# Squares for an overflow check, and the high parts of split numbers, given to other engines and other places in a planned kernel

## The chip, the cores and the metric

The kernel runs on one core of a Trainium2 chip. The core has TensorE (PE), VectorE (DVE), ScalarE (ACT) and GpSimd (POOL), and SyncE (SP), whose queue issues nearly all DMAs here. The metric is the device time of one execution in microseconds.

## The reference

Attention with capped scores for 4 batches of 12 heads, 448 positions and 64 features, and then a gated two-layer product on its output, all in fp32:

```python
scores = scale * np.matmul(q, k.transpose(0, 1, 3, 2))
scores = cap * np.tanh(scores / cap)
attn = softmax(scores)                   # along the keys, 1e-9 added to the sum
x = (attn @ v) as [1792 tokens, 768]
g, val = x @ w_gate, x @ w_val           # [768, 1536]
out = (g * sigmoid(g) * val) @ w_out     # [1536, 768]
```

## The kernel before, in words

Three stages follow each other on TensorE.

*Attention.* 24 pairs of heads, two pairs (a quad) at a time. Per quad TensorE makes seven score tiles in PSUM (`sc`, L884), ScalarE takes tanh (L888) and exp (L891) of each, VectorE adds up (L811, L813), and TensorE multiplies by v (`av`, L829, L910) and sums (L916). The result is copied out of `av` (op `xk`) and later multiplied by reciprocals that travel through DRAM (ops `rl`, `rs`, `rld`; the last is L838 on SP, the product L847 on VectorE, op `x`). That is x, cut into blocks B11, B21, B22 and so on for two halves w of the batches.

*Expert products.* The products are done by a seven-product scheme (p = 1, 2, 6, 5, 7, 3, 4) over sums and differences of blocks. Every fp32 operand is split into a high fp16 part (a cast, ops `XH` for x and `wH` for weights, L259 on VectorE or L257 on ScalarE) and a low one (`XL`, `wL`: the number minus its high part, L264 on VectorE), and each product is three fp16 matmuls (L527 high by high, L528, L529). There are 13 steps over 12 column blocks f; the first has only w = 0, the last only w = 1. Per step ScalarE or VectorE copy banks out of PSUM (`c1`, `cu`, `c5`; tiles c00 to c21), VectorE adds others (`c11`, `c22`, `c12`, L545), ScalarE takes silu (L560, tile `th`), VectorE makes the gated value (`va`, L565), and SP stores it (`hst`, L571, tensor `hidden`).

*Output products.* The gated values are loaded back (`hld`, L614) and go through the same scheme with w_out in two passes (pr = 0, 1), with `oH`, `oL`, `wH`, `wL` as above and matmuls at L702 to L704; L723 adds a bank to a tile, L727 stores the output.

Beside this, ScalarE squares x, the gate weights, w_out and the gated values (op names `qx`, `q`, `qo`, `qh`, all by L322, with the row maximum check `fit` at the end): a check that no fp16 part over- or underflows. Only that check reads the squares.

The order of the instructions on every engine is set beforehand by a planner (class Plan). Each op has a priority, the engines that may do it with a supposed duration on each, the ops it depends on, and the buffers it takes, with the ops that set them free. The planner steps through supposed time, takes the ready op of the best priority, and picks the engine that ends first. So a dependency that is dropped, or an engine that is forbidden, reorders the program around it. A queue works in its order; what stands behind a waiting instruction waits too.

Of the kernel before, what the change touches and what calls it, by code (L numbers as in the profile page):

```python
# [16 lines left out]
P = 128  # L17
# [62 lines left out]
class Plan:  # L80
# [9 lines left out]
    ISSUE = {"rld": 0.96}  # L90
    LAND = {}
    BIAS = {}
# [12 lines left out]
    def run(self):  # L105
# [69 lines left out]
        while ready:  # L175
# [20 lines left out]
            if e == "SP":  # L196
                b = max(s + 1.125, dma_free)
                free[e] = s + self.ISSUE.get(k[0], 0.48)
                dma_free = b + d
                end[k] = dma_free + 0.73 + self.FAR.get(k[0], 0.0)  # L200
            else:
                free[e] = s + d
                end[k] = s + d
                end[k] += self.LAND.get(k[0], 0.0)
                if e == "PE":
                    last = kind(k)
# [17 lines left out]
def tile_capped_attention_gated_mlp(ctx: ExitStack, tc: tile.TileContext, qd, kd, vd, cap, eye, w1, w2, out):  # L224
# [198 lines left out]
    def blocks(w):  # L423
        g0, g1 = 2 * w * NCC, (2 * w + 1) * NCC
        for c in range(HALF):
# [14 lines left out]
            for p, (_, _, _, z) in PROD.items():  # L440

                def high(e, z=z, c=c):
                    T["xs", z, w, c] = x_half(("XH", z, w, c), home(z, w, c))
                    copy(e, T["xs", z, w, c][:, 0], T["raw", z, w, c])

                def low(e, z=z, c=c):
                    sub(e, T["xs", z, w, c][:, 1], T["raw", z, w, c], T["xs", z, w, c][:, 0])

                raw = ("x", {"B11": g0 + c, "B21": g0 + c + HALF, "B22": g1 + c + HALF}[z]) if z[0] == "B" else (z, w, c)
                order = prod_at[w, w, p] - AHEAD + 0.3 * c  # L450
                op(("XH", z, w, c), order, {"ACT": 0.57, "DVE": 0.39} if w else {"DVE": 0.39}, high, [raw], [(home(z, w, c), [("p", LAST[w], w, p)])])
                op(("XL", z, w, c), order + 0.01, {"DVE": 0.62}, low, [("XH", z, w, c)])
                if z in PLAIN:
                    square(("qx", z, w, c), 2, order + 3.0, 0.58, lambda z=z, c=c: T["raw", z, w, c], [raw], ("XH", z, w, c))

    def step(s):
# [46 lines left out]
        for half in range(2):  # L503
            if 0 in ws:
                square(key("q", half), 0, at[0] - 6.0 + 2.0 * half, 0.85, lambda half=half: gate(half).rearrange("p a b -> p (a b)"), full[half], ("XH", "B11", 0, 0))
        last = [2, 5, 3, 4]
        for n in range(4):
            tw = at[n] - 8.8
            k = 1.0 if n < 3 else 0.5
            deps = [full[0], [key("S", 2)], [key("S", 4)], full[1]][n]  # L510
            use = [("p", s, w, last[n]) for w in ws]
            op(key("wH", n), tw, {"ACT": 0.85 * k, "DVE": 0.56 * k}, lambda e, n=n: wH(e, n), deps, [(wtag(4 * s + n), use)])
            op(key("wL", n), tw + 1.0, {"DVE": 0.95 * k}, lambda e, n=n: wL(e, n), [key("wH", n)])

        for w in ws:
# [32 lines left out]
            at_ = lambda p, w=w: done[w, p]  # L548
            op(k("c1"), at_(1), both, lambda e, g=keep: g(e, 0, "b2"), [("p", s, w, 1)], [(f"c0{cw(w)}", [("hst", 2 * w, f)])])
            op(k("c11"), at_(2), {"DVE": 0.62}, lambda e, g=plus: g(0, "b1"), [("p", s, w, 2), k("c1")])  # L550
            op(k("cu"), at_(6), both, lambda e, g=keep: g(e, 1, "b2"), [("p", s, w, 6)], [(f"c1{cw(w)}", [("hst", 2 * w + 1, f)])])
            op(k("c5"), at_(5), both, lambda e, g=keep: g(e, 2, "b3"), [("p", s, w, 5)], [(f"c2{cw(w)}", [key("va", w, 1)])])
# [3 lines left out]
            for b in range(2):  # L556
# [40 lines left out]
    def hslot(pr, i, b, c):  # L597
        users = {
            (0, 0): [("oT", pr, "T4", c), ("oL", pr, 6, c)], (0, 1): [("oT", pr, "T2", c), ("oL", pr, 5, c)],
            (1, 0): [("oL", pr, 4, c)], (1, 1): [("oT", pr, "T2", c), ("oL", pr, 3, c), ("qh", pr, 1, 1, c)],  # L600
        }[i, b]
# [3 lines left out]
    def outs(pr):  # L605
# [15 lines left out]
        for i, b in ((0, 0), (1, 0), (0, 1), (1, 1)):  # L621
            for c in range(HALF):
# [38 lines left out]
        for n, (p, d) in enumerate(OUT_ORDER):  # L661
# [112 lines left out]
    def pair(u, q):  # L774
# [33 lines left out]
        def sadd(e, n):  # L808
# [438 lines left out]
```

## Time and profile before

| | us |
|---|---|
| median of 3 runs | 612.39 |
| lowest and highest | 612.13, 613.45 |
| the profiled execution, as timed | 613.15 |
| its span, first to last instruction | 611.1 |
| TensorE busy in it | 592.3 |
| VectorE, ScalarE busy | 509.6, 405.1 |

The three stages take TensorE to about 168, 460 and 605 us of the span. An engine's busy share is a mean over stages with different limits, so the rows below go by stretches.

### The profile page before, as it was taken

How to read it: one execution, taken by the hardware profiler on the slowest of the kernel's cores; microseconds unless marked ns; L12 is line 12 of the kernel's file. 1: busy time of each engine (PE TensorE's matmuls, PEld its weight loads, DVE VectorE, ACT ScalarE, POOL GpSimd, SP SyncE). 2: the span in 40 equal slices, each digit the busy share in tenths (PEclk: the TensorE clock that was granted, in tenths of full speed). 3: DMA queues.
4: the chain of work that ended last, by engine and by line, in shares of the span. 5: the costliest groups of instructions: out<-in, count | busy, mean ns of one | idle time of the engine just before them, and what ended most of it. 6: DMA issues, size and time to landing. Idle time of an engine off the chain costs nothing.

```text
span 611.1 us, 9532 instructions
## 1 busy us (share of the span) xinstructions
PE 592.3 (97%) x3333; PEld 279.6 (46%) x3333; DVE 509.6 (83%) x878; ACT 405.1 (66%) x669; POOL 1.5 (0%) x11
## 2 busy tenths in 40 slices
PE   7999999999897999999999999999999899999995
PEld 2333333333353455555555555555555455555552
DVE  2779899996998999788989989897969998998830
ACT  6999999999786755545455464452768977953311
POOL 1000000000000000000000000000000000000000
PEclk9999999999999999999999999999999999999998
DMA  8586588664313355878777687767578689644111
GB/s 254 203 243 192 175 232 236 192 171 143 95 40 109 127 168 160 251 221 235 226 242 219 202 248 228 220 200 245 224 248 297 211 285 318 192 147 153 48 61 65
DMA packets 69453, 118.07 MB, mean 193 GB/s; under 512 B 13588, under 2 KB 47380, under 8 KB 69397
## 3 DMA queue, kind: packets, MB, share of 16 engines
q1 hardware_dynamic: 69362, 117.38, 61.8%
q8 instruction: 28, 0.46, 0.3%
q14 instruction: 29, 0.23, 0.1%
q0 software_dynamic: 32, 0.00, 0.0%
q10 hardware_dynamic: 2, 0.00, 0.0%
HBM read 81.79 MB, written 35.48 MB: 192 GB/s over the span
## 4 chain that ended last, share of the span: by engine, by line
PE 90%; DVE 5%; ACT 2%; DMA 1%; issue 1%; SPq 0%; ACTq 0%
PE b L527 10%; PE b L528 10%; PE b L529 10%; PE sc L884 10%; PE av L829 9%; PE b L704 7%; PE b L703 7%; PE b L702 7%; PE om L529 4%; PE om L527 4%; PE om L528 4%; PE b L916 2%; DVE B L264 2%; PE av L910 2%; DMA wf<-w 1%; PE om L704 1%
## 5 line engine op out<-in xcount | busy, mean ns | idle before, releaser
L527 PE MATMUL b<-A,w 128*128 128x448 f16 x252 | 88.8, 353 | 1.8 <-ACT c L257 1.5
L528 PE MATMUL b<-A,w 128*128 128x448 f16 x252 | 88.8, 352 | 1.1 <-DVE w L264 1.1
L529 PE MATMUL b<-A,w 128*128 128x448 f16 x252 | 88.8, 352 | 0.0
L527 PEld LDWEIGHTS <-w 128*128 128x128 f16 x504 | 49.3, 98 | 49.9 <-issue 3.4
L528 PEld LDWEIGHTS <-w 128*128 128x128 f16 x504 | 49.3, 98 | 48.8 <-issue 1.8
L529 PEld LDWEIGHTS <-w 128*128 128x128 f16 x504 | 49.3, 98 | 45.9
L257 ACT ACTIVATE c<-b 128x448 f32<-128x448 f32 x54 | 28.9, 536 | 45.1 <-PE b L704 25.3
L529 PE MATMUL om<-B,w 128*128 128x448 f16 x144 | 50.7, 352 | 0.4 <-DVE B L264 0.4
L527 PE MATMUL om<-B,w 128*128 128x448 f16 x144 | 50.8, 352 | 0.0
L528 PE MATMUL om<-B,w 128*128 128x448 f16 x144 | 50.8, 352 | 0.0
L884 PE MATMUL sc<-c,c 64*128 64x448 f32 (+1 forms) x192 | 44.9, 572 | 1.7 <-ACT w L888 1.7
L264 DVE TENSOR_TENSOR A<-A,A 128x448 f16<-128x448 f32 (+3 forms) x55 | 44.5, 828 | 1.1 <-ACT A L257 0.9
L257 ACT ACTIVATE wf<-w 128x384 f32<-128x384 f32 x37 | 20.7, 559 | 36.7 <-DMA w<-w 35.9
L888 ACT ACTIVATE w<-sc 128x896 f32<-128x896 f32 x42 | 36.9, 918 | 7.8 <-PE sc L884 7.6
L545 DVE TENSOR_TENSOR c<-c,b 128x448 f32<-128x448 f32 x60 | 37.0, 617 | 5.6 <-PE b L529 3.8
L264 DVE TENSOR_TENSOR w<-B,w 128x768 f16<-128x768 f32 x39 | 37.0, 954 | 3.4 <-ACT w L257 3.2
L704 PE MATMUL b<-B,w 128*128 128x448 f16 x108 | 38.1, 352 | 1.8 <-DVE B L264 1.8
L529 PE MATMUL b<-B,w 128*128 128x448 f16 x108 | 38.1, 352 | 1.6 <-DVE B L264 1.6
L888 ACT ACTIVATE B<-sc 128x896 f32<-128x896 f32 x42 | 36.8, 921 | 3.8 <-PE sc L884 3.6
L560 ACT ACTIVATE th<-c 128x448 f32<-128x448 f32 x48 | 26.2, 568 | 18.8 <-DVE c L565 11.4
L891 ACT ACTIVATE B<-B 128x896 f32<-128x896 f32 x42 | 38.3, 959 | 0.1
L891 ACT ACTIVATE w<-w 128x896 f32<-128x896 f32 x42 | 38.2, 956 | 0.0
(134 smaller groups left out, 1240.8 us busy)
## 6 DMA issues: line engine op xcount, KB each, us to landing
w<-w SPq DMA_DIRECT2D x72, 384.0 KB, 3.7
hidden<-c SPq DMA_DIRECT2D x48, 224.0 KB, 2.2
B<-w_S SPq DMA_DIRECT2D x24, 384.0 KB, 3.5
w<-wf SPq DMA_DIRECT2D x16, 384.0 KB, 4.5
B<-w SPq DMA_DIRECT2D x15, 384.0 KB, 5.4
th<-parts SPq DMA_DIRECT2D x48, 112.0 KB, 3.0
A<-hidden SPq DMA_DIRECT2D x12, 448.0 KB, 5.6
B<-hidden SPq DMA_DIRECT2D x12, 448.0 KB, 4.7
```

The costliest lines, as they stand in the source:

```text
L257: nc.scalar.activation(out_, in_, AF.Copy, scale=1.0 if scale is None else scale)
L264: ENG[e].tensor_tensor(out_, a, b, op=ALU.subtract)
L527: nc.tensor.matmul(o, lhsT=wh, rhs=xh, start=first, stop=False, skip_group_check=True)
L528: nc.tensor.matmul(o, lhsT=wl, rhs=xh, start=False, stop=False, skip_group_check=True)
L529: nc.tensor.matmul(o, lhsT=wh, rhs=xl, start=False, stop=end, skip_group_check=True)
L702: nc.tensor.matmul(o, lhsT=wh, rhs=xh, start=first, stop=False, skip_group_check=True)
L703: nc.tensor.matmul(o, lhsT=wl, rhs=xh, start=False, stop=False, skip_group_check=True)
L704: nc.tensor.matmul(o, lhsT=wh, rhs=xl, start=False, stop=end, skip_group_check=True)
L829: nc.tensor.matmul(T["av", u][D * i : D * i + D, :S], lhsT=T["rv", q][:, a : a + D], rhs=t_(own[j])[:, i], start=j == 0, stop=False, skip_ ...
L884: nc.tensor.matmul(z[rows, h, :S], lhsT=T["rk", w][r, keys], rhs=T["rq", w][r], start=True, stop=True)
L888: nc.scalar.activation(T["t", q, i], T["sc", q, i][:, :, :S], AF.Tanh, scale=icapr)
L891: nc.scalar.activation(T["t", q, i], T["t", q, i], AF.Exp, scale=capr)
```

## The change

The squares are taken elsewhere. Those of x read the high parts (fp16) in the middle of the expert products, and no longer hold the fp32 blocks. Those of the gated values are taken from the tiles c right after the gating, 48 half as large ones in place of 24 on what is loaded back, and hold those tiles. Those of the weights of f = 0 are taken in the last step and not in the first; those of w_out in the second output pass and not in the first. The check `fit` stands later. High parts of x for w = 0 may go to ScalarE too; those of the weights of steps 1 and 2 and of the first output pass go to ScalarE alone. The dropped LAND, and ENG[e] made nc.vector, change no instruction.

```diff
-    sq = const.tile([P, 4, 24], F32, name="sq")
+    sq = const.tile([P, 4, 48], F32, name="sq")
...
-        return [], [(tag, [k for y in two for k in [("XL", *y)] + [("qx", *y)] * (y[0] in PLAIN) + [(r, y[1], y[2]) for r in READERS[y[0]]]])]
+        return [], [(tag, [k for y in two for k in [("XL", *y)] + [(r, y[1], y[2]) for r in READERS[y[0]]]])]
...
-                op(("XH", z, w, c), order, {"ACT": 0.57, "DVE": 0.39} if w else {"DVE": 0.39}, high, [raw], [(home(z, w, c), [("p", LAST[w], w, p)])])
+                op(("XH", z, w, c), order, {"ACT": 0.57, "DVE": 0.39}, high, [raw], [(home(z, w, c), [("p", LAST[w], w, p)])])
...
-                    square(("qx", z, w, c), 2, order + 3.0, 0.58, lambda z=z, c=c: T["raw", z, w, c], [raw], ("XH", z, w, c))
+                    n = 3 * PLAIN.index(z) + c
+                    square(("qx", z, w, c), 2, win_at[3] + 10.0 * n + 5.0 * w, 0.58, lambda z=z, c=c: T["xs", z, w, c][:, 0], [("p", 3 + n // 2, 1, 4)], ("XH", z, w, c))
...
-            if 0 in ws:
-                square(key("q", half), 0, at[0] - 6.0 + 2.0 * half, 0.85, ..., full[half], ("XH", "B11", 0, 0))
+            if 1 in ws:
+                square(key("q", half), 0, at[0] - 6.0 + 2.0 * half, 0.85, ..., full[half], ("XH", "B11", s // NFC, 0))
...
-            op(key("wH", n), tw, {"ACT": 0.85 * k, "DVE": 0.56 * k}, ...)
+            op(key("wH", n), tw, {"ACT": 0.85 * k} if s in (1, 2) else {"ACT": 0.85 * k, "DVE": 0.56 * k}, ...)
...
-            op(k("c1"), at_(1), both, ..., [("p", s, w, 1)], [(f"c0{cw(w)}", [("hst", 2 * w, f)])])
+            op(k("c1"), at_(1), both, ..., [("p", s, w, 1)], [(f"c0{cw(w)}", [("hst", 2 * w, f), ("qh", 2 * w, f)])])
...
+                square(("qh", g, f), 3, max(end, z + 2.0) + 1.0, 0.58, lambda b=b, w=w: T["cc", s, w, b], [key("va", w, b)], ("XH", "B11", 0, 0) if s < NFC - 1 else ("oH", 0, 1, 0))
...
-                square(("qh", pr, i, b, c), 3, at[1, 0] + 1.0 + 2.0 * c + (5.0 if i else 0.0), 0.92, ..., [("hld", pr, i, b, c)], ("oH", pr, 2, 0))
...
-            op(("ld", "o", pr, p, d), tp - 24.0, {"SP": 1.09}, load, dep, [(home_, [("wL", "o", pr, p, d)] + [("qo", p, d)] * (not pr))])
-            if not pr:
-                square(("qo", p, d), 1, tp - 6.5, 0.85, ..., [("ld", "o", 0, p, d)], ("oH", 0, p, 0))
+            op(("ld", "o", pr, p, d), tp - 24.0, {"SP": 1.09}, load, dep, [(home_, [("wL", "o", pr, p, d)] + [("qo", p, d)] * pr)])
+            if pr:
+                square(("qo", p, d), 1, tp - 6.5, 0.85, ..., [("ld", "o", 1, p, d)], ("oH", 1, p, 0))
...
-            op(("wH", *key), tp - 7.0, {"ACT": 0.85, "DVE": 0.56}, wH, [("ld", *key)], ...)
+            op(("wH", *key), tp - 7.0, {"ACT": 0.85} if not pr else {"ACT": 0.85, "DVE": 0.56}, wH, [("ld", *key)], ...)
...
-    fit(out_at + len(OUT_ORDER) * 3 * mm_us + 40.0)
+    fit(out_at + len(OUT_ORDER) * 6 * mm_us - 20.0)
```

TensorE's order is the same in both. Lines of the changed file stand one to two lower (L255 is L257 before, L320 is L322).

First, ScalarE at the end of step 0 and the start of step 1: w5, w0 and w2 are high parts of weights, c00 and c20 are copies out of PSUM, sq marks a square. Before:

```order
L257 ACTIVATE B70_1826<-B21_1363 128x448
L257 ACTIVATE c00_1843<-b2_1808 128x448
L322 ACTIVATE B40_1822,sq_76<-B20_1102 128x448
L257 ACTIVATE w5_1850<-ss_1824 128x768
L322 ACTIVATE B70_1826,sq_76<-B21_1363 128x448
L257 ACTIVATE w0_1857<-ss_1838 128x768
L257 ACTIVATE w2_1871<-wf_1847 128x768
L322 ACTIVATE A10_496,sq_76<-wf_1847 128x768
L560 ACT_TABLE_LOAD
L560 ACTIVATE th_1887<-c01_1712 128x448
L322 ACTIVATE A10_496,sq_76<-wf_1855 128x768
L257 ACTIVATE c20_1901<-b3_1875 128x448
```

Now:

```order
L255 ACTIVATE B70_1775<-B21_1362 128x448
L255 ACTIVATE w5_1793<-ss_1769 128x768
L255 ACTIVATE w0_1821<-ss_1773 128x768
L255 ACTIVATE c00_1834<-b2_1809 128x448
L559 ACT_TABLE_LOAD
L559 ACTIVATE th_1850<-c01_1715 128x448
L559 ACTIVATE th_1854<-c11_1747 128x448
L320 ACTIVATE A10_496,sq_76<-c01_1715 128x448
L255 ACTIVATE w2_1874<-wf_1837 128x768
L255 ACTIVATE c20_1888<-b3_1856 128x448
```

The four squares are gone from between, w5 and w0 stand ahead of the copy c00, and a square of a gated value (c01) stands between silu and w2.

Second, VectorE: the high and low parts of x for w = 0, blocks A31, A50 and A51. Before, in the last two quads of attention, among copies out of `av` and block differences:

```order
L264 TENSOR_TENSOR B32_1644<-B50_1232,B30_1225 128x448
L264 TENSOR_TENSOR w4_1639<-wf_1610,w4_1639 128x768
L259 CAST A31_1665<-A51_700 128x448
L264 TENSOR_TENSOR B30_1225<-B30_1225,B12_1095 128x448
L259 COPY c21_1676<-b2_1647 128x224
L259 COPY B31_1472<-av_1615 128x448
L259 COPY B51_1486<-av_1633 128x448
L264 TENSOR_TENSOR A31_1665<-A51_700,A31_1665 128x448
L259 CAST A50_1710<-A52_661 128x448
L259 CAST A51_1714<-A52_661 128x448
L264 TENSOR_TENSOR A50_1710<-A52_661,A50_1710 128x448
L264 TENSOR_TENSOR A51_1714<-A52_661,A51_1714 128x448
```

Now, some 30 us or two quads earlier, behind the sum L812 (L813 before):

```order
L812 TENSOR_TENSOR B72_1380<-B72_1380,w2_1354 128x896
L262 TENSOR_TENSOR A30_1323<-A50_437,A30_1323 128x448
L262 TENSOR_TENSOR A31_1325<-A51_701,A31_1325 128x448
L262 TENSOR_TENSOR A32_1332<-A51_701,A32_1332 128x448
L257 CAST A50_1412<-A52_660 128x448
L257 CAST A51_1416<-A52_660 128x448
L262 TENSOR_TENSOR A50_1412<-A52_660,A50_1412 128x448
L262 TENSOR_TENSOR A51_1416<-A52_660,A51_1416 128x448
L257 CAST B10_1434<-B12_1091 128x448
L257 CAST A52_1436<-w64_1267 128x448
L262 TENSOR_TENSOR B10_1434<-B12_1091,B10_1434 128x448
L262 TENSOR_TENSOR A52_1436<-w64_1267,A52_1436 128x448
```

The conversions and low parts have moved ahead of the last quads' work.

Third, VectorE at the entry into the output products: L723 (now L722) adds the bank `om` to c00, c01 and c10 when the products p = 2, d = 0, 1, 2 are done; B61, B72 and B12 are low parts of the block that product 6 takes. Before:

```order
L723 SCALAR_TENSOR_TENSOR c00_4719<-om_4735,c00_4719 128x448
L264 TENSOR_TENSOR A11_4312<-B62_4564,B11_4545 128x896
L264 TENSOR_TENSOR w1_4774<-B30_4686,w1_4774 128x768
L264 TENSOR_TENSOR B61_4806<-A10_4309,B71_4762 128x896
L723 SCALAR_TENSOR_TENSOR c01_4708<-om_4767,c01_4708 128x448
L264 TENSOR_TENSOR w2_4808<-B31_4698,w2_4808 128x768
L264 TENSOR_TENSOR B40_4547<-B40_4547,A40_4316 128x896
L723 SCALAR_TENSOR_TENSOR c10_4743<-om_4799,c10_4743 128x448
L264 TENSOR_TENSOR A40_4316<-B70_4567,B40_4547 128x896
L264 TENSOR_TENSOR B72_4846<-A11_4312,B41_4797 128x896
L264 TENSOR_TENSOR w3_4842<-B32_4721,w3_4842 128x768
L264 TENSOR_TENSOR B12_4861<-A40_4316,B42_4850 128x896
```

Now:

```order
L262 TENSOR_TENSOR B61_4785<-A10_4347,B71_4762 128x896
L262 TENSOR_TENSOR w0_4777<-B52_4707,w0_4777 128x768
L722 SCALAR_TENSOR_TENSOR c00_4738<-om_4765,c00_4738 128x448
L262 TENSOR_TENSOR B40_4584<-B40_4584,A40_4352 128x896
L262 TENSOR_TENSOR w1_4805<-B30_4740,w1_4805 128x768
L262 TENSOR_TENSOR A40_4352<-B70_4604,B40_4584 128x896
L722 SCALAR_TENSOR_TENSOR c01_4742<-om_4798,c01_4742 128x448
L262 TENSOR_TENSOR B72_4852<-A11_4349,B41_4795 128x896
L262 TENSOR_TENSOR w2_4841<-B31_4774,w2_4841 128x768
L262 TENSOR_TENSOR B12_4872<-A40_4352,B42_4850 128x896
L722 SCALAR_TENSOR_TENSOR c10_4772<-om_4832,c10_4772 128x448
L262 TENSOR_TENSOR w3_4876<-B32_4808,w3_4876 128x768
```

B72 and B12 stood behind the addition to c10 and now stand ahead of it.

## Rows read from the trace of the kernel before

**Rows 1.** Busy time by stretch: stretch, length, engines with instruction counts, clock, DMA share, GB/s.

```profile
168.00:210.00 42.00, 37.25 (x193) 18.56 (x192) 38.51 (x72) 32.98 (x77) 0.00 (x0) 1.00 0.24 78
310.00:430.00 120.00, 120.00 (x636) 62.07 (x635) 107.26 (x207) 57.85 (x112) 0.00 (x0) 1.00 0.74 224
470.00:490.00 20.00, 18.22 (x96) 9.23 (x95) 19.18 (x24) 19.39 (x35) 0.00 (x0) 1.00 0.65 205
605.00:611.20 6.20, 0.00 (x0) 0.00 (x0) 0.00 (x0) 0.51 (x1) 0.00 (x0) 0.67 0.14 46
```

**Rows 2.** Timeline of TensorE: start, length, instruction, idle time before it.

```profile
167.76 0.36 PE L527 MATMUL b<-A,w 128*128 128x448 f16 x1
...
195.50 0.35 PE L527 MATMUL b<-B,w 128*128 128x448 f16 x1
195.69 0.35 PE L528 MATMUL b<-B,w 128*128 128x448 f16 x1
197.42 0.35 PE L529 MATMUL b<-B,w 128*128 128x448 f16 x1 [1.37 <-DVE B L264]
```

**Rows 3.** Waits of TensorE: who waits for whom, total us, times, longest.

```profile
PE b L704 <- DVE B L264: 1.8, 2, 1.2
PE b L529 <- DVE B L264: 1.6, 2, 1.4
PE b L527 <- ACT c L257: 1.5, 1, 1.5
PE sc L884 <- ACT B L888: 1.5, 1, 1.5
PE b L528 <- DVE w L264: 1.1, 1, 1.1
PE om L529 <- DVE B L264: 0.4, 1, 0.4
PE b L527 <- ACT w L257: 0.2, 1, 0.2
```

**Rows 4.** Timeline of ScalarE at the entry into the products.

```profile
156.25 0.84 ACT L257 ACTIVATE w<-ss 128x768 f16<-128x768 f32 x1 [2.71 <-DVE ss L264]
...
182.03 0.57 ACT L322 ACTIVATE B<-B 128x448 f16<-128x448 f32 x1
...
186.67 0.84 ACT L257 ACTIVATE w<-wf 128x768 f16<-128x768 f32 x1 [1.96 <-DMA wf<-w]
...
190.96 0.52 ACT L257 ACTIVATE c<-b 128x448 f32<-128x448 f32 x1
```

**Rows 5.** Timeline of VectorE at the entry into the products.

```profile
141.79 1.15 DVE L811 SCALAR_TENSOR_TENSOR B<-w,eps,w 128x896 f32<-128x896 f32 x1 [2.65 <-PE b L916]
...
160.24 1.15 DVE L259 COPY B<-av 128x448 f32<-128x448 f32 x2
...
166.35 0.39 DVE L259 CAST A<-A 128x448 f16<-128x448 f32 x1 [0.34 <-ACT A L322]
...
196.75 3.29 DVE L264 TENSOR_TENSOR B<-B,B 128x448 f16<-128x448 f32 x6
```

**Rows 6.** Waits of SP, the queue that issues the DMAs.

```profile
SPq L838 <- DVE B L847: 6.5, 1, 6.5
```

**Rows 7.** DMA issues of the page: size of one, median us to landing.

```profile
wf<-w SPq DMA_DIRECT2D x13, 384.0 KB, 4.1
```

**Rows 8.** Timeline of VectorE at the entry into the output products.

```profile
481.75 1.08 DVE L264 TENSOR_TENSOR B<-A,B 128x896 f16<-128x896 f32 x1
```

**Rows 9.** Groups by line and shape: the cast of one weight.

```profile
L259 DVE CAST w<-B 128x768 f16<-128x768 f32 x14 | 7.8, 557 | 3.7 <-PE b L704 3.5 <-DMA B<-w 0.3
...
L257 ACT ACTIVATE w<-B 128x768 f16<-128x768 f32 x25 | 20.9, 835 | 15.8 <-PE b L704 9.8 <-PE om L704 5.3 <-DMA B<-w 0.4
```

**Rows 10.** The page, its first line.

```profile
span 611.1 us, 9532 instructions
```

More of the change, by code (lines that the diff above doesn't have):

```diff
@@ L90 @@
     ISSUE = {"rld": 0.96}
-    LAND = {}
     BIAS = {}
@@ L203, in run @@
                 end[k] = s + d
-                end[k] += self.LAND.get(k[0], 0.0)
                 if e == "PE":
@@ L503, in step @@
         for half in range(2):
-            if 0 in ws:
-                square(key("q", half), 0, at[0] - 6.0 + 2.0 * half, 0.85, lambda half=half: gate(half).rearrange("p a b -> p (a b)"), full[half], ("XH", "B11", 0, 0))
+            if 1 in ws:
+                square(key("q", half), 0, at[0] - 6.0 + 2.0 * half, 0.85, lambda half=half: gate(half).rearrange("p a b -> p (a b)"), full[half], ("XH", "B11", s // NFC, 0))
         last = [2, 5, 3, 4]
@@ L511, in step @@
             use = [("p", s, w, last[n]) for w in ws]
-            op(key("wH", n), tw, {"ACT": 0.85 * k, "DVE": 0.56 * k}, lambda e, n=n: wH(e, n), deps, [(wtag(4 * s + n), use)])
+            op(key("wH", n), tw, {"ACT": 0.85 * k} if s in (1, 2) else {"ACT": 0.85 * k, "DVE": 0.56 * k}, lambda e, n=n: wH(e, n), deps, [(wtag(4 * s + n), use)])
             op(key("wL", n), tw + 1.0, {"DVE": 0.95 * k}, lambda e, n=n: wL(e, n), [key("wH", n)])
@@ L548, in step @@
             at_ = lambda p, w=w: done[w, p]
-            op(k("c1"), at_(1), both, lambda e, g=keep: g(e, 0, "b2"), [("p", s, w, 1)], [(f"c0{cw(w)}", [("hst", 2 * w, f)])])
+            op(k("c1"), at_(1), both, lambda e, g=keep: g(e, 0, "b2"), [("p", s, w, 1)], [(f"c0{cw(w)}", [("hst", 2 * w, f), ("qh", 2 * w, f)])])
             op(k("c11"), at_(2), {"DVE": 0.62}, lambda e, g=plus: g(0, "b1"), [("p", s, w, 2), k("c1")])
-            op(k("cu"), at_(6), both, lambda e, g=keep: g(e, 1, "b2"), [("p", s, w, 6)], [(f"c1{cw(w)}", [("hst", 2 * w + 1, f)])])
+            op(k("cu"), at_(6), both, lambda e, g=keep: g(e, 1, "b2"), [("p", s, w, 6)], [(f"c1{cw(w)}", [("hst", 2 * w + 1, f), ("qh", 2 * w + 1, f)])])
             op(k("c5"), at_(5), both, lambda e, g=keep: g(e, 2, "b3"), [("p", s, w, 5)], [(f"c2{cw(w)}", [key("va", w, 1)])])
@@ L599, in hslot @@
             (0, 0): [("oT", pr, "T4", c), ("oL", pr, 6, c)], (0, 1): [("oT", pr, "T2", c), ("oL", pr, 5, c)],
-            (1, 0): [("oL", pr, 4, c)], (1, 1): [("oT", pr, "T2", c), ("oL", pr, 3, c), ("qh", pr, 1, 1, c)],
+            (1, 0): [("oL", pr, 4, c)], (1, 1): [("oT", pr, "T2", c), ("oL", pr, 3, c)],
         }[i, b]
@@ L626, in outs @@
                    [("hst", g, z), ("hst", g, z + 1)], [hslot(pr, i, b, c)])
-                square(("qh", pr, i, b, c), 3, at[1, 0] + 1.0 + 2.0 * c + (5.0 if i else 0.0), 0.92, lambda i=i, b=b, c=c: T["h", pr, c + HALF * i, b].rearrange("p a s -> p (a s)"), [("hld", pr, i, b, c)], ("oH", pr, 2, 0))
         def va(c, b):
@@ L635, in outs @@
                 ("T3", first, "B22", "B12", [va(c, 1), va(c + HALF, 1)]),
-                ("T1", first + 2.0, "B12", "B11", [("oT", pr, "T3", c), va(c, 0), ("qh", pr, 0, 1, c)]),
-                ("T2", at[1, 0] + 2.0 * c, "B22", "T1", [("oT", pr, "T1", c), ("oL", pr, 1, c), ("qh", pr, 0, 0, c)]),
-                ("T4", at[6, 0] + 2.0 * c, "B21", "T2", [("oT", pr, "T2", c), ("oL", pr, 2, c), ("qh", pr, 1, 0, c)]),
+                ("T1", first + 2.0, "B12", "B11", [("oT", pr, "T3", c), va(c, 0)]),
+                ("T2", at[1, 0] + 2.0 * c, "B22", "T1", [("oT", pr, "T1", c), ("oL", pr, 1, c)]),
+                ("T4", at[6, 0] + 2.0 * c, "B21", "T2", [("oT", pr, "T2", c), ("oL", pr, 2, c)]),
             ):
@@ L673, in outs @@
             dep = [("st", "o", a, d, j) for j in range(2)]
-            op(("ld", "o", pr, p, d), tp - 24.0, {"SP": 1.09}, load, dep, [(home_, [("wL", "o", pr, p, d)] + [("qo", p, d)] * (not pr))])
-            if not pr:
-                square(("qo", p, d), 1, tp - 6.5, 0.85, lambda p=p, d=d: T["wf", "o", 0, p, d].rearrange("p a b -> p (a b)"), [("ld", "o", 0, p, d)], ("oH", 0, p, 0))
+            op(("ld", "o", pr, p, d), tp - 24.0, {"SP": 1.09}, load, dep, [(home_, [("wL", "o", pr, p, d)] + [("qo", p, d)] * pr)])
+            if pr:
+                square(("qo", p, d), 1, tp - 6.5, 0.85, lambda p=p, d=d: T["wf", "o", 1, p, d].rearrange("p a b -> p (a b)"), [("ld", "o", 1, p, d)], ("oH", 1, p, 0))
             def wH(e, p=p, d=d, n=n):
@@ L686, in outs @@
             use = [key + (2,)]
-            op(("wH", *key), tp - 7.0, {"ACT": 0.85, "DVE": 0.56}, wH, [("ld", *key)], [(wtag(4 * len(STEPS) + n), use)])
+            op(("wH", *key), tp - 7.0, {"ACT": 0.85} if not pr else {"ACT": 0.85, "DVE": 0.56}, wH, [("ld", *key)], [(wtag(4 * len(STEPS) + n), use)])
             op(("wL", *key), tp - 6.0, {"DVE": 0.95}, wL, [("wH", *key)])
@@ L812, in sadd @@
             else:
-                ENG[e].tensor_tensor(T["tot", u], T["tot", u], t_(own[2]), op=ALU.add)
+                nc.vector.tensor_tensor(T["tot", u], T["tot", u], t_(own[2]), op=ALU.add)
         op(("sa", u, 0), tile_at(q, own[1]) + 4.0, {"DVE": 1.14}, lambda e: sadd(e, 0), [("exp", q, own[0]), ("exp", q, own[1])], [(["B42", "B72"][upper], [("sum", q)])])
@@ L948, in gates @@
         key = lambda *a: (a[0], "w", s) + a[1:]
-        more = [key("q", half)] * (0 in STEPS[s][1])
+        more = [key("q", half)] * (1 in STEPS[s][1])
         return more + ([key("wH", 0), key("wL", 0), key("S", 2), key("S", 3), key("S", 4)] if half == 0 else [key("wL", 3), key("S", 1), key("S", 3)])
```

## The prediction

> **What bounds the kernel now.** I read the page's busy shares first, then the busy times by stretch, the waits of TensorE, and the timelines of the engines around those waits. TensorE sets the time: in the stretch from 310 to 430 us it is busy for all 120.00 us at a granted clock of 1.00, while VectorE is busy for 107 and ScalarE for 58 [rows 1]. So it can only get shorter where TensorE stands still. One fp16 matmul follows the other after 0.19 us, though each is drawn 0.35 us long [rows 2]. A wait therefore costs about 0.16 us more than the idle time in its row: the one at 197.42 is drawn as 1.37 idle, but its matmul starts 1.73 us after the one before, a loss of 1.54.
>
> The waits come in four groups [rows 3]. (1) On the first tanh tiles, at the start, which the change doesn't touch. (2) 1.5 us on a tanh of the last head pairs (ACT B L888). (3) Entry into the expert products, from 168 to 210 us: 1.6 (twice), 1.5, 1.1, 0.4 and 0.2, which is 4.8 idle in six places, so 4.8 + 6 x 0.16 = 5.8 us. (4) Entry into the output products: 1.8 in two places, so 2.1 us. Behind the last matmul lie 6.2 us of copy, store and end [rows 1]. The most that can be won is 1.5 + 5.8 + 2.1 = 9.4 us. In groups 3 and 4 the neighbours are nearly full: VectorE 38.5 of 42 us and ScalarE 33.0; then 19.2 and 19.4 of 20 [rows 1].
>
> **The change part by part.** *Squares of x.* Now 24 squares of 0.57 us [rows 4] read the fp32 blocks, and a block's buffer stays taken until its square is done. VectorE has to wait for one before the conversion at 166.35, while it stood idle for 2.65 us at 141.79 [rows 5]. In the changed order the conversions of A50, A51 and A52 and the low parts behind them stand about two quads earlier (second excerpt of the order), where that gap is: with A31 four casts of 0.39 and four lows of 0.62, and 0.08 less each back to back (six in a run take 3.29 [rows 5]), some 3.3 us that VectorE no longer has in group 3. ScalarE loses about 20 squares there and takes up some casts of blocks instead.
>
> *Group 3, the waits of 0.2 and 1.1.* They are the high and low parts of w5. ScalarE made w5 only behind a copy out of PSUM that waits for TensorE, and the square at 182.03 [rows 4]. In the changed order w5 and w0 stand ahead of that copy (first excerpt). From the copies out of av at 160.2 [rows 5], as now, to the sum that w5 is made from, VectorE has 18 instructions of 0.53, 4 of about 0.47, 2 of 0.87, two large ones of about 1.0 and three short ones, 16 us (sizes by their elements), and 1 us of waits for TensorE, so about 177; w5 is whole at about 179. With products from about 167.4 (167.76 now [rows 2]) of 9 x 0.19 = 1.70 us each, it is wanted after nine of them, at 182.7. Both waits go: 1.6 us with their 0.16.
>
> *The wait of 1.5 on c20.* ScalarE reached that copy at 190.96, since it had waited 1.96 us for weights until 186.67 and then made a square, a table load, a silu and another square [rows 4]. The weights were late because their loads stand in SP's queue behind the four reads of the last pairs' reciprocals, which waited 6.5 us for a normalisation on VectorE [rows 6]. That normalisation now stands before the next weight sums, some 6 us earlier by the same count; so reads and loads go out at about 178, and land 4.1 us later [rows 7], at 182.3. ScalarE then goes table load, two silus, one square of gated values (waiting for its product until about 184.5), w2, and c20 at 186.4 or so, 1.5 us before it is wanted. 1.7 us go.
>
> *The waits of 1.6 and 0.4 on low parts of the second half.* VectorE works through them in a run at 196.75 [rows 5]. Three of the first (B60, B62, B70) now stand 10 to 20 instructions earlier and are done before their product. The next four (B42, B61, B72, B12) stand behind a sum that waits for TensorE; counted on from it they end within 0.1 us of the moment when TensorE wants them. So of these 2.5 us (2.0 and three times 0.16) I leave 0.6 in. Group 3 gives 5.8 - 0.6 = 5.2 us; bounds 3.0 (every low part of the run late by a whole instruction, 0.53 x 4, and a bit) and 5.8.
>
> *Group 2.* A cast of w3 from the weights' second half goes to ScalarE between a tanh and an exp. Its load now stands in SP's queue behind one small store, about 0.9 us later, so tanh and exp wait some 2 us for it; in return the cast of w2, for which ScalarE waits 2.71 us now [rows 4], comes after one more tanh. Counted on, the last scores start 0.2 us before their present time and the products 0.4 us. Bounds: 0.9 us lost, 1.5 won; I take 0.4 won.
>
> *Group 4.* The output's low parts are the late ones: VectorE adds to c10, which waits for TensorE, and only behind that, at 481.75, makes a low part that TensorE wants at once [rows 8]. In the changed order B72 and B12 stand ahead of that addition (third excerpt). Between two such additions, 18 x 0.19 = 3.4 us apart, now stand two low parts or differences, 1.08 long and 1.0 back to back, and a weight of 768 elements where these have 896: 2 x 1.0 + 0.86 = 2.9 us. It fits, since four conversions and copies of about 0.5 us, which stood in front, went to ScalarE. ScalarE has room, having lost the squares of h and w_out in that stretch. I take 2.0 of 2.1; bounds 1.0 and 2.1.
>
> *What is added.* 48 squares of gated values and 24 of x, 0.57 us each, some 41 us, now lie in the 260 us between 210 and 470. ScalarE goes from 48% [rows 1] to about 64% there; TensorE's work hides it. If that cover goes, the price is in the last rival. The squares of w_out go to the second output pass, where each also holds its buffer: planned 6.5 us ahead of its product, it lets the next load land (0.84 and 4.1 us on) 1.6 us ahead, and that weight's cast can't start before the product's own slot comes free, 3.4 us behind. The final check of the squares moves behind the sum of product 7, d = 1, with seven products or 23.8 us left; two small DMAs (at most 4.1 us each [rows 7]) and about 2 us on VectorE take 10. So the last 6.2 us stay.
>
> *A rule against it.* The same weight cast takes 0.56 us on VectorE and 0.84 on ScalarE [rows 9], and by count 13 casts or copies leave VectorE. The Trainium skill ("ScalarE: Activation LUTs", Rules for kernel authors) says to take VectorE and not ScalarE for relu, max, min, add and mul, since VectorE is the faster per element. The trace agrees on the casts' durations. By that rule alone the sum would be 13 x 0.28 = 3.6 us longer, if all of it lay on the path.
>
> *Sum.* 5.2 + 0.4 + 2.0 = 7.6 us. The profiled execution took 613.15 (span 611.1 [rows 10] and 2.05 around it), so 605.55; the runs' median, 612.39, is 0.76 lower than this execution, which gives 604.8.
>
> **The rivals.** *ScalarE takes VectorE's place in groups 2 and 3.* For it: it is at 33 of 42 us there, its casts are longer by 0.28 us, and w3 makes tanh wait for a load. Against it: it loses more squares than it gains casts. Half of group 3 (2.9 us) and 0.9 us in group 2 would be kept or lost: gain 2.9 - 0.9 + 2.0 = 4.0, so 608.4.
>
> *VectorE bounds the entry anyway.* Six of the eight waits of groups 3 and 4 name its low parts (L264, 1.8 + 1.6 + 1.1 + 0.4). If only those that name ScalarE go, 1.5 + 0.2 and two times 0.16, the time is 610.4. Against it: the order shows 3.3 us of its work gone ahead.
>
> *Squares in ScalarE's queue hold up copies: slower.* ScalarE works in order: its 2.71 us at 156.25 were idle though a tanh stood behind [rows 4]. Between 210 and 470 us a square now waits for VectorE's gated product, and behind it stand the copies that free PSUM banks. They have three products, 5.1 us, less 0.52 for the copy [rows 4]. If a square is held longer than 4.6 us, TensorE waits. Price: 1.7 us, as in the one such wait of today, for each of eleven steps that has it. From five steps on it eats the 7.6 us; at six the time is 612.4 + 6 x 1.7 - 7.6 = 615.0; at four or five there is no change. Against it: no wait of TensorE in that stretch now.
>
> The Trainium skill ("TensorE: Matmul & The Clock Gate", Architectural detail) calls ScalarE's and VectorE's queues strictly first in, first out; the idle time at 156.25 agrees, and it is what this last rival needs.
>
> **How the numbers follow.** The forecast 0.64 (its own range 603.4 to 606.6); ScalarE in VectorE's place 0.16; VectorE bounds anyway 0.06; no change, four or five steps held, 0.07; slower 0.07. A difference under 0.2%, 1.2 us, can't be told from none. So faster 0.86, same 0.07, slower 0.07. The range goes from 602.9 (all 9.4 us won) to 609.0 (group 3 at 3.0, group 4 at 1.0, nothing in group 2, with a bit for the second rival).
>
> **What would show it.** In the new profile no wait on c (L257) and at most one short one on B (L264) around the entry into the products; the products starting 0 to 1 us earlier; the weights' loads at about 178 instead of 182.5; no wait on L704 behind L264; 210 to 470 full. It is wrong if TensorE waits in that stretch for a copy by ScalarE, or if the entry has new waits on casts by ScalarE.

## The result, and the profile after

The changed kernel takes 604.90 us (median of four runs, 604.80 to 604.95), the kernel before 612.62 in the same comparison: a ratio of 0.9874, 95% interval 0.9858 to 0.9890. Forecast were 604.8 us and a range from 602.9 to 609.0. So it is faster, and by about the sum that was worked out. The terms of that sum are less good than its total: two of them held, one was won by more, one loss was not foreseen, and 1.1 us in the profile does not belong to the change.

The page's first line, for [rows 10]:

```profile
span 603.1 us, 9584 instructions
```

The waits of TensorE, for [rows 3] (who waits for whom, us in total, times, longest):

```profile
PE sc L883 <- ACT w L887: 3.2, 3, 1.5
PE b L526 <- ACT c L255: 1.2, 1, 1.2
PE sc L883 <- ACT B L887: 0.8, 1, 0.8
PE av L828 <- DVE B L257: 0.4, 1, 0.4
```

Lines are one or two lower than before. The first row is the start, as before. The six rows of groups 3 and 4 (1.8, 1.6, 1.5 on c, 1.1, 0.4, 0.2) are gone. The tanh of the last pairs has 0.8 instead of 1.5; the 0.4 on a copy in those pairs were 0.3 before. New is a wait of 1.2 us on a copy out of PSUM by ScalarE, at 421.04 us.

Busy time by stretch, for [rows 1]:

```profile
168.00:210.00 42.00, 42.00 (x224) 21.72 (x223) 39.13 (x72) 30.84 (x63) 0.00 (x0) 1.00 0.32 102
310.00:430.00 120.00, 118.84 (x629) 61.41 (x628) 106.32 (x204) 74.43 (x172) 0.00 (x0) 1.00 0.71 220
465.00:485.00 20.00, 20.00 (x108) 10.32 (x107) 19.34 (x22) 13.94 (x20) 0.00 (x0) 1.00 0.61 200
597.00:603.20 6.20, 0.00 (x0) 0.00 (x0) 0.00 (x0) 0.33 (x1) 0.00 (x0) 0.86 0.14 46
```

TensorE is full at both entries, at the same VectorE load (39.13 of 42 and 19.34 of 20); ScalarE has gone from 32.98 to 30.84 at the first and from 19.39 to 13.94 at the second, whose stretch is taken 5 us earlier here, as all of it comes sooner. The 6.2 us of tail stay. From 310 to 430 us TensorE now lacks 1.16.

ScalarE at the entry, for [rows 4]:

```profile
151.56 0.52 ACT L255 ACTIVATE w<-wf 128x384 f16<-128x384 f32 x1 [1.58 <-DMA wf<-w]
...
156.10 0.84 ACT L255 ACTIVATE w<-ss 128x768 f16<-128x768 f32 x1
...
175.88 0.84 ACT L255 ACTIVATE w<-ss 128x768 f16<-128x768 f32 x1 [1.41 <-DVE ss L262]
...
184.97 0.54 ACT L255 ACTIVATE c<-b 128x448 f32<-128x448 f32 x1 [0.21 <-PE b L528]
```

The cast of w2 no longer waits (156.10, where 2.71 us were idle); in its place that of w3 waits 1.58 for its load. The high part of w5 is made at 175.88, ahead of the copy c00 that it stood behind, and c20 is copied at 184.97, as soon as TensorE has it.

VectorE, for [rows 5]:

```profile
138.63 0.39 DVE L257 CAST B<-B 128x448 f16<-128x448 f32 x1
138.93 0.39 DVE L257 CAST A<-w 128x448 f16<-128x448 f32 x1
...
140.72 1.15 DVE L810 SCALAR_TENSOR_TENSOR B<-w,eps,w 128x896 f32<-128x896 f32 x1 [0.34 <-PE b L915]
...
192.37 5.97 DVE L262 TENSOR_TENSOR B<-B,B 128x448 f16<-128x448 f32 x11
```

The 2.65 us of idle time at 141.79 are down to 0.34, filled with conversions of x. The run of low parts that began at 196.75 now begins at 192.37, and has eleven in it instead of six.

I add up each profile in the same way. A wait costs the distance between the starts of two matmuls, less 0.19 us. From the first product to the end of the last matmul, before takes 437.2 us, 7.85 of it such losses, so 429.3; the change 430.7 and 1.5, so 429.2. All kernels below come to 429.2 in this way, or to up to 1.7 more, which the column "pace" shows. "Start" is the time at which the third wait of the start ends. In us:

| Kernel | start | first product | entry 168–210 | 210–465 | exit 465–490 | pace | span | ratio to before (95%) |
|---|---|---|---|---|---|---|---|---|
| before | 14.18 | 167.76 | 5.74 | 0 | 2.11 | 0.1 | 611.05 | 1 |
| changed | 13.11 | 166.03 | 0 | 1.52 | 0 | 0 | 603.05 | 0.9874 (0.9858–0.9890) |
| e1 | 13.26 | 165.05 | 3.81 | 0 | 4.04 | 0 | 608.31 | 0.9963 (0.9945–0.9980) |
| e2 | 14.26 | 168.15 | 5.28 | 0.87 | 1.10 | 0.1 | 611.15 | 0.9961 (0.9943–0.9979) |
| e3 | 14.19 | 167.65 | 5.66 | 0 | 2.10 | 0.2 | 611.23 | 1.0005 (0.9984–1.0027) |
| e4 | 14.01 | 165.76 | 2.99 | 1.15 | 2.10 | 1.7 | 609.30 | 0.9943 (0.9926–0.9961) |
| e5 | 13.14 | 165.97 | 0 | 4.08 | 2.98 | 1.7 | 610.63 | 0.9951 (0.9934–0.9967) |
| e6 | 13.92 | 166.66 | 0.83 | 2.92 | 3.11 | 1.5 | 610.49 | 0.9963 (0.9949–0.9976) |
| e8 | 13.18 | 166.01 | 0 | 1.18 | 0 | 0 | 602.81 | 0.9853 (0.9837–0.9870) |
| e9 | 14.19 | 167.19 | 0 | 0.98 | 0 | 0 | 603.73 | 0.9852 (0.9834–0.9869) |
| e10 | 14.39 | 167.07 | 0 | 2.65 | 0 | 1.6 | 606.77 | 0.9885 (0.9866–0.9903) |
| e11 | 14.36 | 167.21 | 0 | 3.62 | 0.87 | 0 | 607.20 | 0.9884 (0.9866–0.9902) |
| e12 | 14.40 | 167.42 | 0 | 0.75 | 0.88 | 0 | 604.67 | 0.9912 (0.9895–0.9928) |
| e13 | 14.19 | 167.21 | 0 | 0.38 | 2.10 | 0 | 605.15 | 0.9893 (0.9847–0.9939) |

Each row is one execution, the ratio comes from all. On the chips of e1 to e13 the kernel before lay between 611.9 and 617.7 us, so a single span says less than the waits in it.

### The profile page after: what moved, and what is told of

Read it like the earlier page. It is cut to its first block, busy times and chain, and to the rows that moved or that the text cites. A ratio compares the mean times of both kernels' runs of the same rounds, so it can differ in the third digit from the quotient of the medians.

```text
span 603.1 us, 9584 instructions
## 1 busy us (share of the span) xinstructions
PE 590.0 (98%) x3333; PEld 279.4 (46%) x3333; DVE 506.6 (84%) x870; ACT 418.1 (69%) x725; POOL 1.6 (0%) x11
## 4 chain that ended last, share of the span: by engine, by line
PE 90%; DVE 3%; DMA 3%; ACT 2%; issue 1%; SPq 0%; ACTq 0%; DVEq 0%
PE sc L883 10%; PE b L526 10%; PE b L527 10%; PE b L528 10%; PE av L828 9%; PE b L703 7%; PE b L701 7%; PE b L702 7%; PE om L526 4%; PE om L528 4%; PE om L527 4%; PE b L915 2%; DMA w<-w 2%; PE av L909 2%; PE om L703 1%; PE om L701 1%
## 5 line engine op out<-in xcount | busy, mean ns | idle before, releaser
L526 PE MATMUL b<-A,w 128*128 128x448 f16 x252 | 88.8, 352 | 1.2 <-ACT c L255 1.2
L528 PE MATMUL b<-A,w 128*128 128x448 f16 x252 | 88.8, 352 | 0.0
L527 PE MATMUL b<-A,w 128*128 128x448 f16 x252 | 88.8, 352 | 0.0
L255 ACT ACTIVATE c<-b 128x448 f32<-128x448 f32 x54 | 28.9, 538 | 44.5 <-PE b L703 22.9
L255 ACT ACTIVATE w<-B 128x768 f16<-128x768 f32 x32 | 26.8, 840 | 23.4 <-PE b L703 17.6
L703 PE MATMUL b<-A,w 128*128 128x448 f16 x108 | 38.1, 352 | 0.0
```

The source lines that it names most:

```text
L255: nc.scalar.activation(out_, in_, AF.Copy, scale=1.0 if scale is None else scale)
L526: nc.tensor.matmul(o, lhsT=wh, rhs=xh, start=first, stop=False, skip_group_check=True)
L527: nc.tensor.matmul(o, lhsT=wl, rhs=xh, start=False, stop=False, skip_group_check=True)
L528: nc.tensor.matmul(o, lhsT=wh, rhs=xl, start=False, stop=end, skip_group_check=True)
L703: nc.tensor.matmul(o, lhsT=wh, rhs=xl, start=False, stop=end, skip_group_check=True)
```

## The experiments

**Each part alone.** e1 takes the squares of x alone:

```
-  ... [("XL", *y)] + [("qx", *y)] * (y[0] in PLAIN) + ...
+  ... [("XL", *y)] + ...
-  square(("qx", z, w, c), 2, order + 3.0, ..., T["raw", z, w, c], [raw], ...)
+  square(("qx", z, w, c), 2, win_at[3] + 10.0 * n + 5.0 * w, ..., T["xs", z, w, c][:, 0], ...)
```

> The kernel before, with one part of the change alone: the squares of x read the fp16 high parts, late, and no longer hold a block's buffer. Theory (the buffers come free sooner, VectorE's conversions move ahead, and that empties the entry into the products): the waits of TensorE from 168 to 210 us fall from 5.8 us to under 1.5, those from 470 to 490 stay at about 2, and the time is 607 to 608.5. Rival (ScalarE's taking over casts is what does it): the waits from 168 to 210 stay above 4 us and the time above 611.

Entry 3.81 and exit 4.04; 611.82 against 613.90 us, 0.37% faster. Both theories miss, the rival by 0.2 us of waits alone. The squares make VectorE's conversions earlier and cut the entry by 1.9, and the last pairs by 1.8 (first product less start: 151.8 instead of 153.6). But the longest wait left, 2.0 us, still names a low part by VectorE:

```profile
PE b L705 <- DVE B L264: 3.7, 2, 3.0
PE b L530 <- DVE B L264: 2.0, 1, 2.0
```

And the exit gives back 1.9 of it: TensorE wants the first late low part 4.7 us earlier than before, and VectorE has it only 2.9 earlier.

e2 gives away the casts alone:

```
-  op(("XH", ...), order, {"ACT": 0.57, "DVE": 0.39} if w else {"DVE": 0.39}, ...
+  op(("XH", ...), order, {"ACT": 0.57, "DVE": 0.39}, ...
+  {"ACT": 0.85 * k} if s in (1, 2) else ...   # high parts of w
+  {"ACT": 0.85} if not pr else ...            # high parts of w_out
```

> The kernel before, with the casts alone given away: high parts of the first half of x may go to ScalarE, the high parts of w in steps 1 and 2 and of w_out in the first pass must. All squares stay where they were. Theory: ScalarE at the entry still has its squares of x, so at most half of the 5.8 us goes and as much may come back as waits on ScalarE; 610 to 613. Rival: 607 to 608.5, with under 1.5 us of waits from 168 to 210.

Entry 5.28, and its longest wait (1.41, or 1.2 of idle time) is on a cast by ScalarE; as the theory has it, casts alone don't empty the entry. The exit loses 1.0 of its 2.1, and 0.87 come back between 255 and 289 us. The median is 611.93 against 613.90, 0.39% faster; the profile, of the longest of its ten executions, has 0.6 us less of waits and no shorter span.

e3 moves only the squares of the gated values and of w_out, and the final check:

> The kernel before, with the squares of the gated values taken where they are made, those of w_out in the second pass and the final check later, and nothing else. Theory: the waits from 470 to 490 (2.1 us) go, those from 168 to 210 stay at 5 to 6 us; 610.3 to 611. Here 48 squares of gated values lie between 210 and 470: if they hold up copies, one wait of about 1.3 us on a copy by ScalarE shows there, as near the last step of the changed kernel. Rival for the exit (the weights' casts on ScalarE are what frees VectorE): 1 to 2 us of waits stay there.

No change (1.0005): the entry keeps 5.66 and the exit 2.10. So the rival for the exit holds: squares taken away from ScalarE there do nothing by themselves. The 48 squares between 210 and 470 cost TensorE nothing here.

e4 is the changed kernel with the casts back:

> The changed kernel with its casts back where they were (first half of x on VectorE alone, weights on either engine); all the squares moved as in the change. Theory: the entry into the products keeps at most 1 us of waits, the output's entry at most 1; 604.5 to 606.5. Rival (the casts do it): 608 or more, with 3 us or more of waits from 168 to 210.

Entry 2.99 and exit 2.10, 611.25 us where at most 606.5 were expected: the theory that the casts hardly count is wrong, and the longest waits are on VectorE's low parts again:

```profile
PE b L528 <- DVE B L262: 2.0, 1, 2.0
PE b L703 <- DVE B L262: 1.1, 1, 1.1
PE b L701 <- ACT B L255: 0.7, 1, 0.7
```

Between 130 and 193 us VectorE makes 14 casts in e1, 13 in e4 and 7 in the changed kernel (6.2, 5.6 and 3.0 us); the 2.6 to 3.2 us between them are more than the 2.0 by which the latest low part came late.

**Two parts together.** e5 has everything for the products and nothing for the output (e1, the casts of x and w of e2, the squares of the weights of f = 0 in the last step and not in the first):

> The kernel before with the parts of the change for the products alone: squares of x late and without a hold, casts of x and of w in steps 1 and 2 given to ScalarE, squares of w one step later. At the output nothing is changed (squares of the gated values and of w_out, casts of w_out, final check as before). Theory (squares of x and casts are needed together for the entry, and the exit has its own cause in the casts of w_out): waits of TensorE from 168 to 210 us under 0.7 us, from 465 to 490 us 3.5 us or more, since TensorE comes sooner and the exit gives back what the entry won; 607 to 609.5 in quiet runs. Rival (the gain of the entry stays whole): the exit stays at 2.1 us; 605.5 to 607.

The entry is empty: squares and casts together do what neither does alone. But the gain is not kept: exit 2.98 (3.5 or more were expected), and 4.08 of new waits from 376 to 453 us that were not expected, so 610.75 us instead of 607 to 609.5. One of them is the wait near 421, in a kernel that has no square of a gated value in that place. Its ScalarE timeline:

```profile
420.24 0.56 ACT L257 ACTIVATE wf<-w 128x384 f32<-128x384 f32 x1 [1.52 <-DMA w<-w]
420.69 0.53 ACT L970 ACTIVATE w<-w 128x384 int32<-128x384 uint16 x1
421.37 0.54 ACT L257 ACTIVATE c<-b 128x448 f32<-128x448 f32 x1
```

The copy that TensorE waits for stands behind a conversion of later weights, which waits for their load.

e6 has the squares of x and all casts, the other squares as before:

> The kernel before with the squares of x late and without a hold, and all the casts given to ScalarE; the squares of w, of the gated values and of w_out and the final check stay as before. Theory (the exit needs ScalarE free of squares as well): entry under 0.7 us of waits; exit 2 to 4 us, waits on casts by ScalarE among them; no wait near 421, since no square of a gated value stands there. Rival (casts alone cure the exit): exit under 1 us; with no wait at 421 that would be a span of 601.5 to 602.5, below the changed kernel's 603.05.

Exit 3.11, with ScalarE at 18.55 of 20 us from 470 to 490: the exit needs its squares gone as well as the casts given. Both waits there name a low part by VectorE, though I had expected casts by ScalarE among them; that ScalarE's squares hold VectorE up is argued from ScalarE's load and not shown:

```profile
PE b L705 <- DVE B L264: 2.8, 2, 2.1
```

I also expected no wait near 421, and it is there (1.25). And 0.83 are left at the entry, in two waits for VectorE at 169 and 186 us, where e5 has none. At the entry e5 differs by the squares of the weights of f = 0, so these too seem to count.

e13 undoes one line of the changed kernel:

```
-  {"ACT": 0.85} if not pr else {"ACT": 0.85, "DVE": 0.56}, wH, ...
+  {"ACT": 0.85, "DVE": 0.56}, wH, ...
```

> The changed kernel, with the high parts of w_out in the first pass back on either engine, as the planner likes; all else as changed. Theory (with the squares out of the way, it is these casts on ScalarE that let VectorE have the output's low parts in time): entry empty, 421 as in the changed kernel, exit 1 to 2.2 us of waits on VectorE's low parts; span 604 to 605.5. Rival (the casts of x and w at the entry are enough): exit under 0.3 us, span as the changed kernel's, 603 to 603.8.

Exit 2.10, entry empty, span 605.15 with the later start:

```profile
PE b L703 <- DVE B L262: 1.1, 1, 1.1
PE b L701 <- ACT B L255: 0.7, 1, 0.7
```

This is the exit's whole term, brought back by that line, as forecast; only one of its two waits names VectorE, the other a cast by ScalarE. That the wait at 421 falls to 0.38 was not forecast.

**The wait at 421 us.** e8 issues none of the 96 squares and keeps the order of all else (the final check reads a constant):

> The changed kernel with none of its 96 squares issued, every other instruction in the same order; the final check then reads a constant in their place. Theory: the squares cost TensorE only the wait at 421 us (1.3 us), so that wait goes, entry and exit stay empty, and the span is 1.2 to 2 us shorter than the changed kernel's (the start of the attention, 0 to 1 us by execution, left out). Rival (the squares hold up more than that, the waits in the last head pairs at 158 and 159 us too): 2.5 us or more shorter.

The wait at 421 goes, but 1.18 come at 431, on a copy out of the other batch pair's bank. That copy stands in ScalarE's queue behind three casts for the output, whose gated values are loaded back late (1.51 us idle before the second, at 428.00). All the squares together cost 0.3 us of waits, and the span is 0.24 shorter: less than either theory gave.

e9 is the changed kernel unaltered, beside the next three:

> The changed kernel unaltered, for the same chip and rounds as the next three, and to see whether the start and the wait at 421 us belong to the kernel or to one execution. Theory: the wait at 421 comes again (1.2 to 1.6 us in all from 210 to 465), entry and exit stay empty; the attention starts either as in the changed kernel's profile or up to 1.1 us later, whichever kernel runs.

The wait came again, at 421.85 and a little smaller than expected (0.98), the entries are empty, and the start is the late one. Its five runs lie between 604.0 and 606.1 us.

e10 moves two squares:

```
-  [key("va", w, b)], ("XH" ...
+  [key("va", w, b)] + [("c1", 11, 0)] * (s == 10 and w == 1), ("XH" ...
```

> The changed kernel with the two squares of w = 1 in step 10 put behind the copy c1 of step 11. Theory (a late weights' load holds up the region; the squares only decide where it shows): the wait at 421 falls under 0.4 us, but 0.5 to 1.2 us show up at a later copy between 425 and 435; the sum over 210 to 465 falls from 1.5 to 0.6 to 1.2 us. Rival (the squares alone are the cause): the waits from 210 to 465 vanish, 1.3 to 1.5 us shorter.

Slower than the changed kernel (606.83 against 604.66; each ratio lies outside the other's interval). Both theories miss: the wait at 421 is gone, but one of 2.25 (2.09 of idle time) stands at 433.61; ScalarE there, just ahead of the copy:

```profile
428.48 0.95 ACT L255 ACTIVATE A<-A 128x896 f16<-128x896 f32 x1 [2.43 <-DMA A<-hidden]
429.93 0.95 ACT L255 ACTIVATE A<-A 128x896 f16<-128x896 f32 x1 [0.50 <-DMA A<-hidden]
431.71 0.95 ACT L255 ACTIVATE A<-A 128x896 f16<-128x896 f32 x1 [0.84 <-DMA A<-hidden]
432.57 0.56 ACT L559 ACTIVATE th<-c 128x448 f32<-128x448 f32 x1
433.04 0.53 ACT L255 ACTIVATE c<-om 128x448 f32<-128x448 f32 x1
```

As in e8, the copy stands behind three casts for the output, each waiting for gated values (`hidden`) to be loaded back.

e11 sets `NARROW_STEP_B` from 7.4 to 7.0, which plans the later weights' conversions sooner; e12 has both edits.

> The changed kernel with the quarters of the later weights planned 7.0 instead of 7.4 us apart, so that the last loads and their conversions stand earlier in all queues; squares as in the change. Theory (the late load is the cause): waits from 210 to 465 fall to 0.5 us or less; entry and exit stay empty; span 1 to 1.5 us below the changed kernel's. Rival (squares alone): the wait near 421 stays at 1 us or more.

> The two edits before together: squares behind the copy, and quarters 7.0 us apart. Theory: no wait of TensorE over 0.2 us from 168 to 490 us, span 601.5 to 602 with the start of the changed kernel's profile; the fastest of all. Rival: it gives 0.3 us at most against the kernel with the earlier quarters alone.

Neither helps. e11 has no wait at 421 but five others, three of them on additions by VectorE (1.9 us of idle time), one on a copy by VectorE and 0.9 at the exit: it seems that sooner conversions take VectorE's time elsewhere. e12's profiled execution, the shortest of its six, has 0.75 and 0.88; its median is 608.09, above the changed kernel's. No version here beats the changed kernel while it does all of its work.

## Why the prediction was right, and where not

In the profiles the span falls by 8.00 us: start 1.07, last pairs 0.66, entry 5.74, exit 2.11 and pace 0.1 won, 1.52 lost from 210 to 465, and 0.2 lost in the tail. Forecast were 0.4 + 5.2 + 2.0 = 7.6.

*Entry (5.2 forecast, 5.74 measured).* The steps came as put: w5's high part before the copies, SP's reads of the reciprocals and the weights' first load sooner (issued at 175.6, forecast 178, of which 1.1 is the start), c20 at 184.97 (forecast 186.4). The 0.6 us that I left in for low parts of the second half were not there in this nor in any kernel with both parts (e5, e8 to e13). What the prediction didn't separate is that the squares alone win 1.9 and the casts alone 0.5, and that only both win all of it (with 0.83 left in e6, where the weights' squares stay). "VectorE bounds the entry anyway", one of the rivals, is what e1 shows: every wait that is left there names VectorE.

*Last pairs (0.4 forecast, 0.66 measured, 0.58 in e9).* By first product less start. The mechanism was right: without any of the casts given away (e1, e4) it is 1.8 won, so they cost 1.1 to 1.2 here. The one that stands in this place, as the prediction said, is that of w3, which waits 1.58 us for its load between a tanh and an exp; a version without it alone was not run.

*Exit (2.0 forecast, 2.11 measured).* Right in size, and e13 ties it to the casts of w_out on ScalarE. One step of the working was wrong and did no harm: it counted 2.9 us of VectorE's work between two additions 3.4 us apart and left out the addition itself. With its 0.54 us nothing is to spare; in the new profile the additions start at 467.40, 470.81 and 474.21, and VectorE has no idle time between them. e6 and e3 show that casts and moved squares are needed together; the prediction had ScalarE's room from the squares and VectorE's from the casts.

*From 210 to 465 (0 forecast, 1.52 lost).* This step failed, and by the prediction's own sign: it was to be wrong if TensorE waits in that stretch for a copy by ScalarE. The prediction gave a copy three products, 5.1 us, before TensorE wants its bank. In step 11, as in steps 0 and 1 (`SKEWED = (0, 1, 11)` in the kernel), the products of one batch pair follow each other directly, so that only one product, 1.7 us, lies between the first and the one that adds on in its bank and needs its copy. There the mechanism of the slower rival appears, once instead of in eleven steps. The changed kernel's ScalarE:

```profile
414.85 0.58 ACT L968 ACTIVATE w<-w 128x384 int32<-128x384 uint16 x1 [3.31 <-DMA w<-w]
...
418.19 0.56 ACT L320 ACTIVATE A<-c 128x448 f16<-128x448 f32 x1
418.66 0.19 ACT L320 ACTIVATION_READ_ACCUMULATOR A<-c 128x1 f32 x1
419.19 0.58 ACT L320 ACTIVATE A<-c 128x448 f16<-128x448 f32 x1 [0.34 <-DVE c L564]
419.67 0.19 ACT L320 ACTIVATION_READ_ACCUMULATOR A<-c 128x1 f32 x1
419.89 0.58 ACT L320 ACTIVATE A<-c 128x448 f16<-128x448 f32 x1
420.37 0.19 ACT L320 ACTIVATION_READ_ACCUMULATOR A<-c 128x1 f32 x1
420.46 0.52 ACT L255 ACTIVATE c<-b 128x448 f32<-128x448 f32 x1
```

Three squares stand before the copy, and they wait for gated values that VectorE made late. The chain of waits leads further back, to a load that VectorE's queue waits for:

```profile
414.79 0.36 DVE L259 TENSOR_SCALAR wf<-w 128x384 f32<-128x384 f32 x1 [2.23 <-DMA w<-w]
```

```profile
409.43 5.34 DMA w<-w
414.79 0.36 DVE wf L259
...
418.56 0.55 DVE c L564
419.19 0.68 ACT A L320 x2
420.00 0.37 issue
420.56 0.44 ACT c L255
421.04 0.35 PE b L526
```

A load of the last weights takes 5.34 us (the median of such loads is 3.8), and VectorE's queue, with the gated products behind the conversion, stands for 2.2 of them. In e9 and e13, where TensorE asks for this bank 1.2 us later than here, the chain has these loads in the same place, and 0.98 and 0.38 us are lost, first e9, then e13:

```profile
412.77 4.92 DMA w<-w
```

```profile
413.42 3.69 DMA w<-w
```

So the squares hand a delay on: without them the wait at 421 goes (e8), but e5 and e6 have it with none of these squares, and in e8 and e10 another stands one bank later, behind casts that wait for other loads. The kernel before has none, with TensorE 7.5 us later at that place (1.73 + 5.74); e3, with the squares and TensorE as late, has none either. What it would take to remove it stays open: the two edits tried moved it.

*Start (1.07, no part of the change).* e9 is the same kernel with the start of the kernel before. Its first scores against those of the changed kernel's first profile, first e9's, then the other:

```profile
4.64 2.66 PE L883 MATMUL sc<-c,c 64*128 64x448 f32 x8
```

```profile
4.40 1.77 PE L883 MATMUL sc<-c,c 64*128 64x448 f32 x8
```

The same eight matmuls take 2.66 or 1.77 us. So by the profiles' spans the change is worth 8.0 − 1.1 = 6.9 us, 0.7 under the forecast: 0.9 more from the three terms won, 1.5 less by the wait, 0.1 less by pace and tail. That the time hit 604.8 to 0.1 us is partly luck. Nor is 6.9 a fixed figure: on e9's chip the medians lie 9.4 us apart (614.08 and 604.66), with the late start in the profile, and no profile of the kernel before was kept there that could say why.

*ScalarE against VectorE for casts.* The rule quoted against the change (3.6 us if all casts lay on the path) did not decide: with them taken back (e4) 5.1 us of waits return at the two entries. ScalarE has the room and VectorE not: from 168 to 193 us of e4 ScalarE stands idle for 10.3 us and VectorE for 2.0.

## What to carry to other kernels

When several engines are nearly full at an entry, take two reliefs apart and together before crediting one: here neither the freed buffers nor the moved casts emptied it, and both did. A gain ahead of a second bottleneck is only kept if that one is relieved too (e1, e5: the exit's waits grew by 1.9 and 0.9 us). Before work goes into an in-order queue, look for the place with the least slack behind it, not the usual one: one step in another order was enough.

## What the runs showed of the hardware

At the start, the distance of two warm-up matmuls is 0.37 us, and the first scores go partly at that pace or all at twice it, from one execution to the next of one kernel (2.66 and 1.77 us above). The clock column reads 1.00 there in both, but the trace's first clock record, at the higher level, 2.4 GHz, begins only at 4.10 us in the changed kernel's first profile and at 6.47 in e9's; before it there is none. Over the fourteen profiles it begins at 4.1 to 4.4 us in five, and in four of these the start ends by 13.3 (the fifth, e6, waits 0.6 us for a load); in the other nine it begins at 6.0 to 6.9, and the start ends at 14.0 to 14.4. The Trainium skill ("TensorE: Matmul & The Clock Gate", What's actually happening) says that the matmul at which the clock rises differs from run to run of one kernel; the two profiles agree.

A wait in mid-run can cost twice. In e10, behind 2.09 us of waiting, the granted clock falls to the lower level, 1.2 GHz (0.50), and the products run at that pace for some 3 us, which is the 1.6 under "pace":

```profile
432.00:434.00 2.00, 0.39 (x2) 0.17 (x2) 1.40 (x4) 2.00 (x5) 0.00 (x0) 0.89 1.05 421
434.00:436.00 2.00, 2.00 (x7) 0.82 (x6) 2.00 (x5) 1.87 (x6) 0.00 (x0) 0.50 0.98 342
436.00:438.00 2.00, 2.00 (x10) 0.91 (x8) 2.00 (x4) 0.85 (x2) 0.00 (x0) 0.76 0.49 186
438.00:440.00 2.00, 2.00 (x13) 1.00 (x11) 1.63 (x3) 2.00 (x4) 0.00 (x0) 1.00 0.66 197
```

The same happened in e4 (after 2.0 us of waiting), e5 and e6, and not in e1, whose wait of 3.01 at 480.00 left the clock at 1.00. What decides between them, these runs don't show.
